# 96 further matmuls behind the last FFN tile of a transformer block

## The chip, the cores and the metric

The kernel runs on one core of a Trainium2 chip. The metric is the device time of one execution in microseconds (us); every time below comes from the profile of one execution or from the timed runs.

## What is computed

A block that adds three things: its input, an attention over 8 earlier positions at stride 2, and a feed-forward network (FFN) with a squared ReLU. S is 2048 rows, D is 576, the hidden width F is 4608, all in float32.

```
xn  = layernorm(x)
q, k, v = split(xn @ wqkv)                  # 32 heads of 18
logits[s, w] = q[s] . k[s - 2 w] / sqrt(18) # w = 0..7, earlier positions alone
attn = softmax(logits over w)
A   = (sum over w of attn[s, w] v[s - 2 w]) @ wo
h   = xn @ w1 + b1
B   = relu(h)**2 @ w2 + b2
out = x + A + B
```

## The kernel before

[...] To keep accuracy, every operand is split into a high and a low half, and each product is made of three matmuls: high by high, high by low, low by high. The copies that make the halves run on ScalarE (ACT) and VectorE (DVE); the lines of the profile for them are L96 (high half) and L98 (low half).

The rows are worked through in four blocks of 512 (`NB = 4`, `TB = 512`), and in each block the FFN runs over 36 tiles of 128 hidden units (`NF = 36`), so 144 tiles in all (`NT = 144`). `step(n)` deals with tile n:

- it asks for the weights of tile n + 2 (`load_w`, on the queue of SyncE) and splits the first weight of tile n + 1 (`split_w1`);
- `ffn1(n)` makes the hidden units: 14 matmuls of 128 x 512 into one PSUM tile `wk` (L340), then ReLU and square on ACT (L342, L345, L346) and the low half `hl` on DVE (L347);
- `split_w2(n)` splits the second weight into `w2h` and `w2l`;
- `ffn2(n - LAG)` adds a finished tile to six PSUM banks `y0` to `y5` that hold the block's result, with pairs of matmuls of 320 and 256 columns (L365). `LAG` is 2, so the second half of a tile is two steps behind its first half.

Between these, the steps carry pieces of the attention, the products with `wo` and the loads of the next block, at hand-written step numbers. The order on each engine is that in which the program states it.

Behind step 143 there is one more, step 144, which runs `ffn2_tail` for the last two tiles. It takes the banks `y0` to `y5` one after another: six matmuls (L365, twelve for a bank of two halves), then `drain` on DVE (L385) adds the bank to the input rows, and a store to the output follows (L404, L406, L408). The last bank, `y5`, is therefore the last to be computed, drained and stored.

Buffers come from rotating pools: `w1h` and `w1l` have 2 buffers each, `w2h` 3, `hh` 4, `raw1` 3, and the PSUM pool of `wk` 2. A tile that takes a buffer over waits until the last reader of its former tile is done. A float32r matmul loads its stationary operand itself, so each shows up as one weight load (PEld) and one matmul (PE). A bf16 matmul is preceded by a weight load of its own. In the kernel before there are 14 bf16 matmuls, all at its start (L448), on a tile of zeros.

Of the kernel before, what the change touches and what calls it, by code (L numbers as in the profile page):

```python
# [8 lines left out]
F32 = mybir.dt.float32  # L9
F32R = mybir.dt.float32r  # L10
BF16 = mybir.dt.bfloat16
AF = mybir.ActivationFunctionType
# [4 lines left out]
P = 128  # L17
S, D, F = 2048, 576, 4608
H, DH, W, DIL = 32, 18, 8, 2
TB = 512  # L20
NB = S // TB
NJ = TB // P
NC = 5
# [16 lines left out]
def block_kernel(ctx: ExitStack, tc: tile.TileContext, x, xt, wqkv, wo, w1, b1, w2, b2, out):  # L40
# [453 lines left out]
    def step(n):  # L494
        if 2 < n + 2 < NT:
            load_w(n + 2)
        if n + 1 < NT:
            split_w1(n + 1)
        for f, a in pre.get(n, []):
            f(*a)  # L500
        if n < NT:
            ffn1(n)
            split_w2(n)
        busy = n >= NF and n % NF in (LAG - 1, LAG - 2)
        for f, a in mid.get(n, []):
            f(*a)
        if not busy:
            piece()
            piece()
        if n == NT:  # L510
            ffn2_tail([NT - 2, NT - 1])
        elif n >= LAG:
            ffn2(n - LAG)
        if not busy:
            piece()

    for n in range(NT + 1):
        with opening() if n < 3 else ExitStack():
            step(n)


_OUTS = [((1, S, D), 'float32')]

# [33 lines left out]
```

## Time and profile before

| | |
|---|---|
| median of the timed runs | 1196.32 us (1195.88 and 1196.75) |
| the profiled execution, its time | 1196.13 us |
| its span, first to last instruction | 1194.1 us |
| TensorE matmuls (PE) busy | 1185.2 us, 99% |
| TensorE weight loads (PEld) busy | 1077.8 us, 90% |
| VectorE (DVE) busy | 869.2 us, 73% |
| ScalarE (ACT) busy | 597.5 us, 50% |
| granted TensorE clock, mean | 1.000 of full speed |

The profiled execution's time is 2.03 us longer than its span, and 0.19 us below the median of the runs. Matmuls are pipelined: one starts before the end of the one before it, so the duration of a single matmul is longer than the distance from start to start. Where a row of the timeline merges several instructions, it shows the stretch from the first start to the last end.

### The profile page before, as it was taken

What the parts mean: (1) busy time and instruction counts of PE and PEld (TensorE: products, weight loads), DVE (VectorE), ACT (ScalarE), POOL (GpSimd) and SP (SyncE); (2) the same over time, 40 slices, a digit from 0 to 9 for tenths busy, and PEclk for the clock granted to TensorE, in tenths of its full rate; (3) what the DMA queues carried; (4) which work ended last, traced back from release to release, by engine and by line L of the source; (5) the groups of instructions that cost most, each with busy time, mean ns of one, the idle gap of its engine ahead of it and who ended that gap; (6) DMA issues with size and microseconds to landing.
All of it is one profiled execution on the core that took longest, in us unless ns stands there. A gap on an engine that the chain in (4) does not pass through costs nothing.

```text
span 1194.1 us, 17735 instructions
## 1 busy us (share of the span) xinstructions
PE 1185.2 (99%) x6930; PEld 1077.8 (90%) x6930; DVE 869.2 (73%) x1051; ACT 597.5 (50%) x1079; POOL 40.7 (3%) x47
## 2 busy tenths in 40 slices
PE   8999999999999999999999999999999999999998
PEld 5998998989898989989989899989998999998998
DVE  7499798882689795994288979598428895958432
ACT  6546445553546454555354545455535454445541
POOL 4002000000000200000000020000000000000000
PEclk9999999999999999999999999999999999999999
DMA  7546345332536544433264654533326434343311
GB/s 233 196 169 227 127 148 201 100 99 73 198 129 213 207 163 152 132 91 109 72 230 138 230 203 119 179 96 105 102 87 225 178 109 169 99 153 95 106 60 50
DMA packets 70164, 172.22 MB, mean 144 GB/s; under 512 B 8384, under 2 KB 20288, under 8 KB 69312
## 3 DMA queue, kind: packets, MB, share of 16 engines
q1 hardware_dynamic: 70080, 171.09, 43.4%
q8 instruction: 54, 0.88, 0.3%
q14 instruction: 30, 0.25, 0.1%
HBM read 156.81 MB, written 14.24 MB: 143 GB/s over the span
## 4 chain that ended last, share of the span: by engine, by line
PE 97%; DVE 2%; ACT 0%; DMA 0%; issue 0%; SPq 0%; POOL 0%
PE y L365 42%; PE wk L340 39%; PE wk L239 15%; DVE xt L183 1%; PE wk L200 1%; DVE w2l L98 0%; DMA xb<-in_x 0%; SPq L87 0%; DVE wql L98 0%; PE y L200 0%; DVE hl L347 0%; ACT r L342 0%; ACT hh L345 0%; DVE st L109 0%; DVE w1l L98 0%
## 5 line engine op out<-in xcount | busy, mean ns | idle before, releaser
L365 PE MATMUL y<-w2h,hh 128*128 128x256 f32 (+1 forms) x1152 | 253.0, 297 | 0.0
L365 PE MATMUL y<-w2l,hh 128*128 128x256 f32 (+1 forms) x1152 | 252.9, 296 | 0.0
L365 PE MATMUL y<-w2h,hl 128*128 128x256 f32 (+1 forms) x1152 | 251.9, 296 | 0.0
L340 PE MATMUL wk<-xh,w1h 128*128 128x512 f32 x720 | 215.6, 396 | 0.9 <-DVE kv L205 0.9
L365 PEld LDWEIGHTS y<-w2h,hh 128*128 128x128 f32 x1152 | 186.1, 189 | 9.2
L340 PE MATMUL wk<-xh,w1l 128*128 128x512 f32 x720 | 191.4, 394 | 2.0 <-DVE w1l L98 2.0
L365 PEld LDWEIGHTS y<-w2l,hh 128*128 128x128 f32 x1152 | 180.7, 190 | 2.2
L365 PEld LDWEIGHTS y<-w2h,hl 128*128 128x128 f32 x1152 | 179.6, 190 | 0.4
L96 ACT ACTIVATE w1h<-raw 128x640 fp32r<-128x640 f32 x144 | 105.9, 736 | 124.4 <-PE wk L340 113.8
L340 PEld LDWEIGHTS wk<-xh,w1l 128*128 128x128 f32 x720 | 134.7, 187 | 35.3 <-DVE w1l L98 2.3
L96 ACT ACTIVATE w2h<-raw 128x576 fp32r<-128x576 f32 x144 | 98.1, 683 | 135.1 <-PE y L365 133.9
L340 PE MATMUL wk<-xl,w1h 128*128 128x512 f32 x576 | 158.1, 394 | 0.0
L98 DVE TENSOR_TENSOR w1l<-raw,w1h 128x640 fp32r<-128x640 f32 x143 | 119.4, 835 | 52.7 <-PE wk L340 37.3
L98 DVE TENSOR_TENSOR w2l<-raw,w2h 128x576 fp32r<-128x576 f32 x144 | 112.6, 783 | 53.6 <-ACT w2h L96 53.4
L340 PEld LDWEIGHTS wk<-xh,w1h 128*128 128x128 f32 x720 | 126.0, 188 | 22.0 <-DVE kv L205 1.1
L301 DVE TENSOR_REDUCE qo<-pr 128x144 f32<-128x1152 f32 x64 | 139.7, 2183 | 0.6
L340 PEld LDWEIGHTS wk<-xl,w1h 128*128 128x128 f32 x576 | 107.6, 187 | 26.3
L347 DVE TENSOR_TENSOR hl<-r,hh 128x512 fp32r<-128x512 f32 x144 | 100.0, 694 | 34.5 <-ACT r L346 34.4
L342 ACT ACTIVATE r<-wk,b1t 128x512 f32<-128x512 f32 x144 | 98.7, 686 | 49.1 <-PE wk L340 48.9
L98 DVE TENSOR_TENSOR wql<-wqr,wqh 128x432 fp32r<-128x432 f32 x80 | 48.9, 628 | 98.0 <-ACT wqh L96 98.0
L239 PE MATMUL wk<-wql,xh 128*128 128x432 f32 x320 | 115.0, 360 | 0.0
L239 PE MATMUL wk<-wqh,xh 128*128 128x432 f32 x320 | 114.4, 358 | 0.0
(77 smaller groups left out, 1229.2 us busy)
## 6 DMA issues: line engine op xcount, KB each, us to landing
raw<-in_w SPq DMA_DIRECT2D x144, 320.0 KB, 2.9
raw<-in_w SPq DMA_DIRECT2D x144, 288.0 KB, 2.8
wqr<-in_wqkv SPq DMA_DIRECT2D x80, 216.0 KB, 4.4
kv<-kscr SPq DMA_DIRECT2D x16, 1008.0 KB, 5.7
kv<-vscr SPq DMA_DIRECT2D x16, 1008.0 KB, 7.8
raw<-in_wo SPq DMA_DIRECT2D x20, 288.0 KB, 2.7
kscr<-kv SPq DMA_DIRECT2D x16, 288.0 KB, 3.0
vscr<-kv SPq DMA_DIRECT2D x16, 288.0 KB, 3.4
```

What stands on the lines that cost most here:

```text
L96: nc.scalar.activation(hi, raw, AF.Copy)
L98: (only or nc.vector).tensor_tensor(out=lo, in0=raw, in1=hi.bitcast(F32), op=ALU.subtract)
L183: nc.vector.tensor_tensor(out=v, in0=v, in1=mb[b][:, :, k].rearrange("c p j -> c j p"), op=op)
L200: nc.tensor.transpose(p[:, j * P:(j + 1) * P], src[:, j, c * P:(c + 1) * P], ident)
L239: nc.tensor.matmul(ps, l, r, start=i == 0, stop=i == len(mm) - 1)
L301: nc.vector.tensor_reduce(out=q[:, j], in_=pr.rearrange("p w c -> p c w"), axis=AX.X, op=ALU.add)
L340: nc.tensor.matmul(p, l, r, start=i == 0, stop=i == len(mm) - 1)
L342: nc.scalar.activation(r, p, AF.Relu, bias=b1t[:, f:f + 1])
L347: last_hl[0] = nc.vector.tensor_tensor(out=hl, in0=r, in1=hh.bitcast(F32), op=ALU.subtract)
L365: nc.tensor.matmul(y, a[:, t * P:(t + 1) * P], w[:, c0:c1], start=first and i == 0 and opens, stop=last and i == len(pairs) - 1, skip_grou ...
```

## The change

A function `rate_rows` is called once, behind the last step. It makes four copies of the last tile's first weight, which still lies in its buffer: on ACT into a `w1h` and a `w2h` buffer, on DVE into a `w1l` buffer (which nothing reads) and, as bf16, into an `hh` buffer. It takes the two `wk` tiles of PSUM, `a` and `c2`, and issues 96 matmuls into them. Nothing reads their results, and each overwrites the one before it. The matmuls come in groups: 38 of 512 columns with fixed or changing stationary and moving operands, 4 of 512 columns with every second element, 4 each of 320, 256, 128, 64 and 32 columns, two groups of 4 of 256 columns at different starts, 4 in bf16, and at the end 8 full ones of 512 columns mixed with 14 that use only the lower or the upper 64 rows of the array.

```diff
+    def rate_rows():
+        b = NB - 1
+        wh = sb.tile([P, NC * P], F32R, name="w1h", bufs=2)
+        wl = sb.tile([P, NC * P], F32R, name="w1l", bufs=2)
+        m2 = sb.tile([P, D], F32R, name="w2h", bufs=3)
+        nc.scalar.activation(wh, raw1[NT - 1], AF.Copy)
+        nc.vector.tensor_copy(wl, raw1[NT - 1])
+        nc.scalar.activation(m2, raw1[NT - 1][:, :D], AF.Copy)
+        low = sb.tile([P, TB], BF16, name="hh", bufs=4)
+        nc.vector.tensor_copy(low, raw1[NT - 1][:, :TB])
+        a = pw.tile([P, TB], F32, name="wk")
+        c2 = pw.tile([P, TB], F32, name="wk")
+        cs = lambda c: slice(c * P, (c + 1) * P)
+        x_, l_ = xh[b], xl[b]
+        mm = lambda p, l, r: nc.tensor.matmul(p, l, r, start=True, stop=True, skip_group_check=True)
+        for i in range(6):
+            mm(a, wh[:, cs(0)], x_[:, 0])
+        for i in range(8):
+            mm(a, wh[:, cs(i % 4)], x_[:, 0])
+        for i in range(8):
+            mm(a, wh[:, cs(0)], x_[:, i % 4])
+        for i in range(8):
+            mm(a, wh[:, cs(i % 4)], x_[:, i % 4])
+        for i in range(8):
+            mm(a, wh[:, cs(i % 4)], l_[:, i % 4])
+        for i in range(4):
+            mm(a, wh[:, cs(i % 4)], x_[:, 0:2].rearrange("p c (n s) -> p (c n) s", s=2)[:, :, 0])
+        for n in (320, 256, 128, 64, 32):
+            for i in range(4):
+                mm(a[:, :n], wh[:, cs(i % 4)], m2[:, :n])
+        for i in range(4):
+            mm(a[:, :256], wh[:, cs(i % 4)], m2[:, 320:])
+        for i in range(4):
+            mm(a[:, :256], wh[:, cs(i % 4)], m2[:, 256:512])
+        for i in range(4):
+            mm(a, low[:, cs(i % 4)], low)
+        h0, h1 = slice(0, 64), slice(64, 128)
+        for i in range(4):
+            mm(a, wh[:, cs(0)], x_[:, 0])
+            mm(a, wh[h0, cs(1)], x_[h0, 1])
+            mm(c2, wh[h1, cs(1)], x_[h1, 1])
+        for i in range(3):
+            mm(a, wh[:, cs(0)], x_[:, 0])
+        for i in range(3):
+            mm(a, wh[h0, cs(1)], x_[h0, 1])
+            mm(c2, wh[h1, cs(1)], x_[h1, 1])
+        mm(a, wh[:, cs(0)], x_[:, 0])
+
+    rate_rows()
```

## The prediction

> **What bounds the kernel now.** I read the page's first and second parts, then the chain of work that ended last, then that chain in order of time near the end, and last the timeline of the final microseconds.
>
> ```profile
> span 1194.1 us, 17735 instructions
> PE 1185.2 (99%) x6930; PEld 1077.8 (90%) x6930; DVE 869.2 (73%) x1051; ACT 597.5 (50%) x1079; POOL 40.7 (3%) x47
> PE 97%; DVE 2%; ACT 0%; DMA 0%; issue 0%; SPq 0%; POOL 0%
> ...
> 1174.90 0.65 PE y L365 x5
> 1175.55 3.27 PE wk L340 x14
> 1178.82 11.72 PE y L365 x88
> 1190.55 0.02 issue
> 1190.57 0.49 DVE xb L385
> ```
>
> The chain is TensorE for 97% of the span, and TensorE is idle for only 1194.1 - 1185.2 = 8.9 us in all. In the last 15 us the chain is one unbroken run of matmuls, and after it come only the drain of the last bank and its store. So whatever is put behind the last matmul on TensorE starts at once, and is on the path that sets the end as soon as it outlasts drain and store. The time of the change is therefore a sum over 96 matmuls, less what drain and store cover.
>
> **Where the added matmuls start, and what covers them.** With the instructions of both programs, as built, laid side by side, nothing changes on TensorE up to the last L365 matmul: the 96 stand behind it in the order of the source. POOL and SyncE issue the same work as before, and no DMA is added. The end of the timeline, and the DMA issue that ends last, are these:
>
> ```profile
> 1190.08 0.31 PE L365 MATMUL y<-w2l,hh 128*128 128x320 f32 x1
> ...
> 1190.22 0.31 PE L365 MATMUL y<-w2h,hl 128*128 128x320 f32 x1
> ...
> 1191.09 0.34 SPq L408 DMA_DIRECT2D out<-xb  x1
> ...
> out<-xb SPq DMA_DIRECT2D x2, 160.0 KB, 2.1
> ```
>
> The last matmul starts at 1190.22; at the pace of its kind (0.147 us, below) the first added one starts at 1190.37. The last store is issued at 1191.09 and takes 2.1 us to land, so at 1193.2. From there to the end of the span are 1194.1 - 1193.2 = 0.9 us, which I take as the closing work of the program: something has to finish last, and then the engines meet. After the change the last matmul finishes last, and I put the same 0.9 us behind it. Drain and store run beside the added matmuls. They cover the stretch from 1190.37 to 1193.2, 2.8 us.
>
> **The pace of a matmul.** A row's mean is the duration of one matmul; what counts in an unbroken run is the distance between starts. These rows give both:
>
> ```profile
> 1183.97 0.31 PE L365 MATMUL y<-w2h,hh 128*128 128x320 f32 x1
> ...
> 1184.85 0.40 PE L365 MATMUL y<-w2h,hh 128*128 128x256 f32 x2
> 1185.09 0.40 PE L365 MATMUL y<-w2l,hh 128*128 128x256 f32 x2
> ...
> 1162.12 0.60 PE L200 MATMUL wk<-ident,qo 128*128 128x128 f32 x4
> ...
> 1.24 6.10 PE L448 MATMUL wk<-warm 128*128 128x512 bf16 x14 [1.24 <-DVE warm L445]
> ...
> L340 PE MATMUL wk<-xh,w1h 128*128 128x512 f32 x720 | 215.6, 396 | 0.9 <-DVE kv L205 0.9
> L365 PE MATMUL y<-w2h,hh 128*128 128x320 f32 x576 | 180.5, 313 | 0.0
> L365 PE MATMUL y<-w2h,hh 128*128 128x256 f32 x576 | 161.2, 281 | 0.0
> L200 PE MATMUL wk<-ident,qo 128*128 128x128 f32 x80 | 12.0, 272 | 0.0
> L448 PE MATMUL wk<-warm 128*128 128x512 bf16 x14 | 6.1, 628 | 1.2 <-DVE warm L445 1.2
> ```
>
> - 512 columns: 14 matmuls of L340 fill 3.27 us of the chain, 0.2336 us each, though one lasts 396 ns. In these 14 both operands change and all write the same bank.
> - 320 columns: six in a row into one bank start from 1183.97 to 1184.85, 0.147 us each.
> - 256 columns: two start between 1184.85 and 1185.09, 0.120 us each.
> - 128 columns: four transposes, (0.60 - 0.272) / 3 = 0.109 us each. This is the narrowest the trace has.
> - bf16 of 512 columns: (6.10 - 0.628) / 13 = 0.421 us at the start of the program. The window below shows the clock at 1.00 at the end, where float32r of the same width takes 0.2336. I take 0.2336 for bf16 too; its lower bound is half of 0.421, 0.210, if the first matmuls ran at half speed.
>
> ```profile
> 1175.00:1190.00 15.00, 15.00 (x105) 14.35 (x104) 3.86 (x7) 2.64 (x4) 0.00 (x0) 1.00 0.09 38
> ```
>
> **The sum, group by group.**
>
> - 38 of 512 columns with fixed or changing operands: 38 x 0.2336 = 8.88. Every float32r matmul here brings a weight load of its own (6930 of each on the page), so I expect no gain from a fixed stationary operand. The lower bound is the 14 that repeat it at 0.210: 0.33 less.
> - 4 with every second element: 4 x 0.2336 = 0.93. No row has a moving operand with a gap. At worst twice the bytes are passed over at the same rate: 0.93 more. I take the plain row, because the columns are the same in number.
> - 4 of 320: 0.59. 12 of 256, whatever their start: 1.44.
> - 12 of 128, 64 and 32 columns at 0.109: 1.31, taking the narrowest row as a floor set by the weight load, which stays 128 x 128. If time fell with the columns, the 256 row gives 4 x (0.060 + 0.030 + 0.015) = 0.42, so 0.89 less; if a narrow one cost as much as the 512 row, 12 x 0.2336 = 2.80, so 1.49 more.
> - 4 in bf16: 0.93, or 0.09 less.
> - 8 full ones among the half-height ones: 1.87.
> - 14 of half height: 14 x 0.2336 = 3.27. No row has a matmul of 64 array rows; the nearest is the full one of the same 512 columns. Lower bound: the two of a pair run at once in the two halves of the array, 7 x 0.2336 = 1.64. Upper bound: full and half height alternate 10 times (twice in each of four rounds, then twice more), and if the array has to empty each time, the part of the 396 ns that overlap hides, 396 - 234 = 162 ns, shows: 1.62 more.
>
> Together 8.88 + 0.93 + 0.59 + 1.44 + 1.31 + 0.93 + 1.87 + 3.27 = 19.22 us. The last matmul starts 0.23 before the end of that sum and lasts 0.396, so TensorE ends at 1190.37 + 19.22 + 0.16 = 1209.75. With the 0.9 us of closing work the span is 1210.65; the profiled execution's time was 1196.13 - 1194.1 = 2.03 us above its span, so the time is 1212.7 us. That execution stands 0.19 us below the median of the runs shown, 1196.32, so against the median it is 16.4 us or 1.4% more.
>
> The Trainium skill, "TensorE: Matmul & The Clock Gate", Back-to-back issue gap, gives columns / 2.4 + 2.5 ns from start to start on a warm array, so 216 ns for 512 columns. This trace does not agree: 0.2336 us, 8% more. By the page the 68 full-width ones would be 68 x 0.018 = 1.2 us cheaper, an estimate.
>
> **The copies.** Four are added, and none is waited for.
>
> ```profile
> L96 ACT ACTIVATE w1h<-raw 128x640 fp32r<-128x640 f32 x144 | 105.9, 736 | 124.4 <-PE wk L340 113.8
> L96 ACT ACTIVATE w2h<-raw 128x576 fp32r<-128x576 f32 x144 | 98.1, 683 | 135.1 <-PE y L365 133.9
> L98 DVE TENSOR_TENSOR w1l<-raw,w1h 128x640 fp32r<-128x640 f32 x143 | 119.4, 835 | 52.7 <-PE wk L340 37.3
> ...
> 1169.23 0.69 ACT L342 ACTIVATE r<-wk,b1t 128x512 f32<-128x512 f32 x1 [2.59 <-PE wk L340]
> 1171.28 0.69 DVE L347 TENSOR_TENSOR hl<-r,hh 128x512 fp32r<-128x512 f32 x1 [3.85 <-ACT r L346]
> ...
> 1180.24 0.63 ACT L346 ACTIVATE r<-r 128x512 f32<-128x512 f32 x1
> 1180.91 0.69 DVE L347 TENSOR_TENSOR hl<-r,hh 128x512 fp32r<-128x512 f32 x1 [3.85 <-ACT r L346]
> ```
>
> The `w1h` copy (0.74 us) stands on ACT ahead of the L342 at 1169.23 and waits for the last matmul of its buffer's former tile. ACT is idle for 2.59 us there. If it came late by its whole length, `hh` and `hl` behind it would slip by 0.74 us, and they are wanted only in the tail after 1183.97, 12 us later. The `w1l` copy on DVE (at most 0.84, the row with two sources) stands ahead of the `hl` at 1171.28 and has 3.85 us of idle time; it waits for matmuls that end near 1169.2. The bf16 copy lies in the 3.85 us ahead of 1180.91. The `w2h` copy (0.68) is the last on ACT and waits for its buffer's last reader, just before 1183.97, so it ends near 1184.7. The first matmul that reads it is the 43rd added one, at 1190.37 + 42 x 0.2336 = 1200.2. That is 15 us of cover; without it TensorE would stand for 0.68 us.
>
> **The rivals.**
>
> *Half-height pairs run at once.* Same sum with 1.64 in place of 3.27: 1211.1 us. For it: the two use different rows of the array and different PSUM tiles, and nothing reads either. Against it: in all of the trace each matmul waits for its forerunner to stream. The Trainium skill, "TensorEngine Tiling (Array Packing)", Key Properties, says that tiles of the array run independently, and that a change of tiling mode first drains the array; by the first half the pairs overlap, by the second the ten changes cost something. No row of before shows either.
>
> *The unusual shapes cost more.* Narrow ones at 2.80, gaps at twice, ten emptyings: 1.49 + 0.93 + 1.62 = 4.04 more at most, 1216.7 us; half of it is 1214.7. For it: no row shows any of them. Against it: all three would have to go the bad way.
>
> *Nothing overlaps* (the one that ends slower by over 2%). Each added matmul opens and closes its own accumulation and writes over the one before it in the same bank. If each had to wait until its forerunner has left the array, full durations would count: 68 x 0.396 + 4 x 0.313 + 12 x 0.281 + 12 x 0.272 = 34.8 us in place of 19.2, so 1228.1 us. It decides from a mean of 0.278 us per matmul on (19.22 + 7.5 to the 2% line, over 96). Against it: the 14 bf16 ones at the start are of this form, and start 0.421 us apart while each lasts 0.628.
>
> *The matmuls end up elsewhere or hidden.* Even if they filled every idle moment of TensorE, 19.2 - 8.9 = 10.3 us would be left, so 1206.4. The order as built speaks against it.
>
> **How the numbers follow.** Forecast by rows 0.48, pairs at once 0.22, unusual shapes dearer 0.24, nothing overlaps 0.04, elsewhere 0.02. The low end takes the pairs at once, the narrow ones by their columns and the fixed operand: 1212.7 - 1.64 - 0.89 - 0.33 = 1209.8, which I round down to 1209.5. The high end is the dear case, 1216.7, and 0.3 us for the engines' meeting: 1217.0. Within 2% of the median means below 1220.2 us, and 2% is about what a measurement of this kernel can tell from no change. All cases but the one without overlap stay below it. Faster is left only 0.01 for what I have not seen, slower 0.05, same 0.94.
>
> **What the changed profile would show.** L535 rows of 96 matmuls with TensorE busy without a gap from about 1190.4 to 1209.7; starts 0.234 us apart in the first 42; the chain ending in PE L535 and no longer in DVE L385; the last store issued at 1191.1 as before; steps up to 1190 the same to a tenth. Wrong would be: a gap ahead of the 43rd (the `w2h` copy late), a pace above 0.278 over the block, a granted clock below 1.00 in it, or two half-height matmuls starting together.

## The result, and the profile after

The changed kernel takes 1213.28 us (two runs, 1213.28 and 1213.29) against 1196.32 before: 17.0 us more, a ratio of 1.0142 with a 95% interval of 1.0098 to 1.0185. That is within 2%, as forecast, and 0.6 us above the forecast of 1212.7.

These are lines of the page, and then the end of the chain of work in order of time:

```profile
span 1211.6 us, 17932 instructions
PE 1205.2 (99%) x7026; PEld 1092.1 (90%) x7026; DVE 869.9 (72%) x1053; ACT 598.6 (49%) x1081; POOL 40.6 (3%) x47
...
1190.34 20.34 PE wk L535 x95
```

TensorE has 96 more matmuls, DVE and ACT two more instructions each. The chain used to end in the drain of the last bank on DVE; now it ends in 20 us of L535. The timeline of TensorE from there on gives the parts of the sum, since each group starts where the one before it has been issued:

```profile
1190.18 7.15 PE L535 MATMUL wk<-xh,w1h 128*128 128x512 f32 x30
...
1197.16 2.03 PE L535 MATMUL wk<-xl,w1h 128*128 128x512 f32 x8
...
1199.03 1.98 PE L535 MATMUL wk<-xh,w1h 128*128 128x512 f32 x4
...
1200.83 3.52 PE L535 MATMUL wk<-w2h,w1h 128*128 128x320 f32 x28
...
1204.19 1.04 PE L535 MATMUL wk<-hh 128*128 128x512 bf16 x4
...
1204.88 5.80 PE L535 MATMUL wk<-xh,w1h 128*128 128x512 f32 x22
```

`float32r`, the type of the kernel's split operands, stands in these rows as f32. A row here merges shapes of one line: the 28 are all those of 320 to 32 columns, the 22 the full and the half-height ones. From start to start:

| part | forecast us | measured us |
|---|---|---|
| start of the first added matmul | 1190.37 | 1190.18 |
| 38 of 512 columns | 8.88 | 8.85 |
| 4 with every second element | 0.93 | 1.80 |
| 28 of 320 to 32 columns | 3.34 | 3.36 |
| 4 in bf16 | 0.93 | 0.69 |
| 8 full and 14 half-height, to TensorE's end | 5.30 | 5.80 |
| end of TensorE | 1209.75 | 1210.68 |
| from there to the end of the span | 0.9 | 0.9 |
| time less span | 2.03 | 1.7 |

The copies cost nothing. These are the two on ACT, in the timeline:

```profile
1167.87 0.74 ACT L526 ACTIVATE w1h<-raw 128x640 fp32r<-128x640 f32 x1 [1.42 <-PE wk L340]
...
1183.97 0.69 ACT L528 ACTIVATE w2h<-raw 128x576 fp32r<-128x576 f32 x1 [3.29 <-PE y L365]
```

The first lies in the gap foreseen, with 0.43 us still idle between it and L342, and the `w2h` copy is done at 1184.7, 16 us before its reader. The two on DVE take 0.49 and 0.42 us, in their gaps.

### The profile page after: what moved, and what is told of

Its sections match the earlier page's. It is cut to its first block, busy times and chain, and to the rows that moved or that the text cites. A ratio compares the mean times of both kernels' runs of the same rounds, so it can differ in the third digit from the quotient of the medians.

```text
span 1211.6 us, 17932 instructions
## 1 busy us (share of the span) xinstructions
PE 1205.2 (99%) x7026; PEld 1092.1 (90%) x7026; DVE 869.9 (72%) x1053; ACT 598.6 (49%) x1081; POOL 40.6 (3%) x47
## 4 chain that ended last, share of the span: by engine, by line
PE 97%; DVE 2%; issue 0%; ACT 0%; DMA 0%; SPq 0%; POOL 0%; DVEq 0%
PE y L365 42%; PE wk L340 38%; PE wk L239 15%; PE wk L535 2%; DVE xt L183 1%; PE wk L200 1%; DVE wql L98 0%; DMA xb<-in_x 0%; SPq L87 0%; PE y L200 0%; DVE w2l L98 0%; DVE hl L347 0%; ACT r L342 0%; ACT hh L345 0%; POOL rs L118 0%
## 5 line engine op out<-in xcount | busy, mean ns | idle before, releaser
L365 PE MATMUL y<-w2h,hh 128*128 128x256 f32 (+1 forms) x1152 | 253.0, 297 | 0.0
L365 PE MATMUL y<-w2l,hh 128*128 128x256 f32 (+1 forms) x1152 | 252.9, 296 | 0.0
L365 PE MATMUL y<-w2h,hl 128*128 128x256 f32 (+1 forms) x1152 | 251.9, 296 | 0.0
L340 PE MATMUL wk<-xh,w1h 128*128 128x512 f32 x720 | 215.6, 396 | 0.9 <-DVE kv L205 0.9
L365 PEld LDWEIGHTS y<-w2h,hh 128*128 128x128 f32 x1152 | 186.1, 189 | 9.2
L340 PE MATMUL wk<-xh,w1l 128*128 128x512 f32 x720 | 191.5, 394 | 2.0 <-DVE w1l L98 2.0
L365 PEld LDWEIGHTS y<-w2l,hh 128*128 128x128 f32 x1152 | 180.7, 190 | 2.2
L365 PEld LDWEIGHTS y<-w2h,hl 128*128 128x128 f32 x1152 | 179.6, 190 | 0.5
L340 PEld LDWEIGHTS wk<-xh,w1l 128*128 128x128 f32 x720 | 134.7, 187 | 35.3 <-DVE w1l L98 2.3
L340 PE MATMUL wk<-xl,w1h 128*128 128x512 f32 x576 | 158.1, 394 | 0.0
L340 PEld LDWEIGHTS wk<-xh,w1h 128*128 128x128 f32 x720 | 126.0, 188 | 21.9 <-DVE kv L205 1.1
L340 PEld LDWEIGHTS wk<-xl,w1h 128*128 128x128 f32 x576 | 107.6, 187 | 26.3
L342 ACT ACTIVATE r<-wk,b1t 128x512 f32<-128x512 f32 x144 | 98.5, 684 | 47.8 <-PE wk L340 47.6
```

The costliest lines, as they stand in the source:

```text
L340: nc.tensor.matmul(p, l, r, start=i == 0, stop=i == len(mm) - 1)
L342: nc.scalar.activation(r, p, AF.Relu, bias=b1t[:, f:f + 1])
L365: nc.tensor.matmul(y, a[:, t * P:(t + 1) * P], w[:, c0:c1], start=first and i == 0 and opens, stop=last and i == len(pairs) - 1, skip_grou ...
```

## Experiments

The theory behind the forecast: the time added is the sum of the paces of the matmuls, less what drain and store cover. Two terms came out dearer and were open: reading with gaps, and changes between full and half height. Every experiment changes `rate_rows` alone. The first five are compared with the kernel before by their times; the others hold groups of matmuls on lines of their own, and are read from their profile, one execution each.

### The changed kernel again

No edit: a base for the next three on the same chip.

> The changed kernel as it is, on the same chip as the three that follow, so that they can be compared with it. Both theories: 1213.3 us, 17.0 over the kernel before.

Measured: 1214.53 us (1213.56 to 1215.37), against 1196.58 for the kernel before on the same chip, ratio 1.0149 (1.0135 to 1.0163). The added part is the same as in the first profile, 20.34 us of the chain. What differs lies 1180 us earlier, and is told in the last section: single executions scatter by 1 to 2 us, so the next two are read from their profiles.

### The same matmuls, sorted by height

```diff
-        for i in range(4):
-            mm(a, wh[:, cs(0)], x_[:, 0])
-            mm(a, wh[h0, cs(1)], x_[h0, 1])
-            mm(c2, wh[h1, cs(1)], x_[h1, 1])
...
+        for i in range(8):
+            mm(a, wh[:, cs(0)], x_[:, 0])
+        for i in range(7):
+            mm(a, wh[h0, cs(1)], x_[h0, 1])
+            mm(c2, wh[h1, cs(1)], x_[h1, 1])
```

> The same 96 matmuls, but the last block in another order: its 8 full ones first, then its 7 pairs of half height. Theory: every change between 128 and 64 rows costs 0.19 us, because the weight load of the next matmul can't run beside the one before; there are 10 changes in the mixed order and 1 in this, so 9 x 0.19 = 1.7 us less than the changed kernel, 1211.6 us. Rival: the half-height matmuls themselves are dear (0.43 us a pair, whatever stands next to it); then the order changes nothing and the time stays 1213.3 us.

The start of the added part and the last block in the timeline of the repeated kernel, and then the last block in that of the sorted one:

```profile
1190.85 7.15 PE L535 MATMUL wk<-xh,w1h 128*128 128x512 f32 x30
...
1205.56 5.80 PE L535 MATMUL wk<-xh,w1h 128*128 128x512 f32 x22
```

```profile
1206.45 4.05 PE L535 MATMUL wk<-xh,w1h 128*128 128x512 f32 x22
```

The block is 1.75 us shorter, and 1.7 were expected: the order costs, and not the half-height matmuls. The time is 1213.51 us, ratio 1.0137 (1.0124 to 1.0151); that is 1.0 less than the repeated kernel, but the intervals overlap, so the time alone doesn't show it.

### The four with gaps read plainly

```diff
-            mm(a, wh[:, cs(i % 4)], x_[:, 0:2].rearrange("p c (n s) -> p (c n) s", s=2)[:, :, 0])
+            mm(a, wh[:, cs(i % 4)], x_[:, i % 4])
```

> The same 96 matmuls, but the four that read every second element read 512 neighbouring ones instead. Theory: the gap alone makes them 0.454 us in place of 0.2336, so 4 x 0.22 = 0.88 us less than the changed kernel, 1212.4 us, and they start 0.23 us apart. Rival: something else slows the matmuls at this place (what is left of the store, a wait for the copy behind them); then they stay 0.45 us apart and the time stays 1213.3 us.

In its timeline the four and the group behind them:

```profile
1201.23 1.10 PE L535 MATMUL wk<-xh,w1h 128*128 128x512 f32 x4
1202.16 3.51 PE L535 MATMUL wk<-w2h,w1h 128*128 128x320 f32 x28
```

The four take 1202.16 - 1201.23 = 0.93 us instead of 1.80: the gap is the whole cause. The time, 1214.18 us (ratio 1.0145, 1.0129 to 1.0160), doesn't resolve 0.87 us.

### Only 8, and only 16 added matmuls

```diff
-        for i in range(6):
-            mm(a, wh[:, cs(0)], x_[:, 0])
...
+        for i in range(8):
+            nc.tensor.matmul(a, wh[:, cs(i % 4)], x_[:, i % 4], start=True, stop=True, skip_group_check=True)
```

> Only 8 added matmuls of 512 columns in place of 96, all four copies kept. Theory: drain and store of the last bank cover what ends before the store lands. TensorE ends at 1190.18 + 8 x 0.2336 + 0.16 = 1192.2 of the span, the store lands at 1192.8, so the time is that of the kernel before, 1196.3 us, and the span 1194.1. Rival: all that stands behind the last L365 matmul adds to the time: 8 x 0.2336 = 1.9 us, 1198.2 us.

> As with 8, but 16 added matmuls of 512 columns. Theory: TensorE ends at 1190.18 + 16 x 0.2336 + 0.16 = 1194.1 of the span, 1.3 us after the store has landed, and the same 0.9 us of closing work follow: span 1195.0, 0.9 us over the kernel before, so 1197.2 us. Rival that all adds: 16 x 0.2336 = 3.7 us, 1200.0 us.

The ends of the two timelines, first with 8, then with 16:

```profile
1190.11 2.02 PE L536 MATMUL wk<-xh,w1h 128*128 128x512 f32 x8
...
1190.83 0.34 SPq L408 DMA_DIRECT2D out<-xb  x1
```

```profile
1190.55 3.88 PE L536 MATMUL wk<-xh,w1h 128*128 128x512 f32 x16
```

With 8, TensorE ends at 1192.1, before the store lands at 1190.83 + 2.1 = 1192.9: the time is 1196.12 us against 1196.58 for the kernel before on that chip, ratio 0.9997 (0.9988 to 1.0005), where the rival asked for 1.9 us more. With 16, TensorE ends at 1194.43 and the span, 1195.3, 0.9 us later: 1198.31 us against 1197.70, ratio 1.0005 (0.9996 to 1.0014). That is 0.6 us more, where the theory had 0.9 and the rival 3.7. Both agree with the cover of the forecast and rule out that all the matmuls add; the interval with 16, -0.5 to 1.7 us, is too wide to size the cover.

### What a gap in the moving operand costs

Groups of 8 with 512 or 256 columns and several patterns. Two of the lines:

```diff
+            nc.tensor.matmul(a, wh[:, cs(i % 4)], xf[:, :2048].rearrange("p (n s) -> p n s", s=4)[:, :, 0], ...)
+            nc.tensor.matmul(a.rearrange("p (n s) -> p n s", s=2), wh[:, cs(i % 4)], xf[:, :1024].rearrange("p (n s) -> p n s", s=4)[:, :, :2], ...)
```

> In place of the 96: groups of 8 matmuls with 512 columns whose moving operand is read plainly, then every 2nd, 3rd and 4th element, then 2 of 4, then 4 of 8, then 4 pieces of 128 from far apart; then 256 columns with every 2nd element and plainly; then bf16 with 512 columns plainly and every 2nd, 256 columns with every 4th and plainly; last plain float32r again. Theory A (time goes with the span of bytes passed over): from start to start 0.23, 0.45, 0.68, 0.91, 0.45, 0.45 us, pieces 0.23; bf16 0.22 and 0.43, 0.43 and 0.11. Theory B (two neighbours of 8 bytes come in one read, and without a neighbour each element needs its own): 0.23, 0.45, 0.45, 0.45, then 0.23 for 2 of 4, 4 of 8 and the pieces; bf16 of 2 bytes with every 2nd may stay at 0.22. Theory C (lines of 16 bytes need two hits): 0.23, 0.23 to 0.45, 0.45 or more, 0.9, and 2 of 4 as plain.

The timeline; a group's pace is the distance to the next row over 8:

```profile
1191.80 2.02 PE L538 MATMUL wk<-xh,w1h 128*128 128x512 f32 x8
1193.66 3.79 PE L540 MATMUL wk<-xh,w1h 128*128 128x512 f32 x8
1197.27 3.78 PE L542 MATMUL wk<-xh,w1h 128*128 128x512 f32 x8
1200.87 3.87 PE L544 MATMUL wk<-xh,w1h 128*128 128x512 f32 x8
1204.56 3.81 PE L546 MATMUL wk<-xh,w1h 128*128 128x512 f32 x8
1208.19 2.05 PE L548 MATMUL wk<-xh,w1h 128*128 128x512 f32 x8
```

Plain (L538) 0.232 us; every second, third and fourth (L540, L542, L544) 0.451, 0.450 and 0.461; 2 of 4 (L546) 0.454; 4 of 8 (L548) fills 2.05 us as the plain ones fill 2.02, and so do the pieces. None of the three theories holds: A fails on the third and fourth and on 4 of 8, B on 2 of 4, C on the fourth and on 2 of 4. In bf16 every second costs 0.226 against 0.217, and 256 columns with every fourth 0.225 against 0.11 plainly (from start to start within the row). So there are two paces, and four elements within 16 bytes seemed to get the good one. The next run tests that:

```diff
+            nc.tensor.matmul(a.rearrange("p (n s) -> p n s", s=4), wh[:, cs(i % 4)], xf[:, :1024].rearrange("p (n s) -> p n s", s=8)[:, :, 2:6], ...)
+            nc.tensor.matmul(a.rearrange("p (n s) -> p n s", s=4), wh[:, cs(i % 4)], xf[:, :768].rearrange("p (n s) -> p n s", s=6)[:, :, :4], ...)
```

> In place of the 96, groups of 8. float32r: 512 columns plainly; plainly, but begun one element later; 4 of 8; 4 of 8 begun two elements later; 4 of 6; 8 of 16 begun two elements later; 2 of 4 begun one later. bf16: plainly; 2 of 4; 256 columns with every third; 4 of 8. Last plain float32r. Theory D, after the run before (each four elements that follow one another run at full pace where they lie in one aligned line of 16 bytes, and at half pace otherwise; unbroken reading excepted): 0.233, 0.233, 0.233, 0.45, about 0.34, 0.34, 0.45; bf16 0.216, 0.216, 0.22, 0.216. Rival E (what counts is a run of 16 bytes, wherever it lies): 0.233 for the first six, 0.45 for 2 of 4; bf16 0.43 for 2 of 4, 0.22 for every third (half pace for 256 columns), 0.43 for 4 of 8.

```profile
1196.07 2.03 PE L542 MATMUL wk<-xh,w1h 128*128 128x512 f32 x8
1197.93 3.79 PE L544 MATMUL wk<-xh,w1h 128*128 128x512 f32 x8
1201.54 2.90 PE L546 MATMUL wk<-xh,w1h 128*128 128x512 f32 x8
1204.27 2.79 PE L548 MATMUL wk<-xh,w1h 128*128 128x512 f32 x8
1206.88 3.80 PE L550 MATMUL wk<-xh,w1h 128*128 128x512 f32 x8
...
1212.26 1.97 PE L554 MATMUL wk<-hh 128*128 128x512 bf16 x8
1214.07 1.53 PE L556 MATMUL wk<-hh 128*128 128x256 bf16 x8
1215.44 1.97 PE L558 MATMUL wk<-hh 128*128 128x512 bf16 x8
```

4 of 8 (L542) takes 0.232, the same begun two elements later 0.451, 4 of 6 0.341, 8 of 16 begun two later 0.326, 2 of 4 begun one later as long a row as L544 with its 0.45, and bf16 with 2 of 4 (L554) 0.226, with 4 of 8 (L558) filling the same 1.97 us. Plain reading begun one element later takes (1196.07 - 1194.18) / 8 = 0.236. D holds in all of these to 0.015 us, and E, which asked for 0.23 in the three float32r groups that D slows and for 0.43 in bf16, fails. D misses one: every third in bf16 takes 0.171 for 256 columns where both said 0.22. The rule is thus good for float32r and not complete for bf16.

### What a change of height costs

Full ones, halves, pairs, quarters and mixtures, each group on a line of its own. One of them, full and lower half by turns:

```diff
+        for p, l, r in [(a, wh[:, cs(0)], x_[:, 0]), (a, wh[h0, cs(1)], x_[h0, 1])] * 6:
+            nc.tensor.matmul(p, l, r, start=True, stop=True, skip_group_check=True)
```

> In place of the 96, on lines of their own: 8 full matmuls; 6 times (full, lower half); 6 times (full, lower half, upper half); 12 lower halves; 12 pairs of lower and upper half; 12 times four quarters of 32 rows into four banks; 8 full; 6 times (3 full, 3 pairs); 8 full. Theory (each change of the number of rows costs 0.19 us, halves of a pair run at once, and nothing else costs): a full one 0.234; a round of full and lower half 2 x 0.234 + 2 x 0.19 = 0.85; a round of full and pair the same 0.85; a lower half 0.234; a pair 0.234; four quarters 0.234; a round of 3 full and 3 pairs 6 x 0.234 + 2 x 0.19 = 1.78. Rival (the second half of a pair is what costs): full and lower half 0.47, full and pair 0.85, pair alone 0.43. Rival (a half-height matmul can't load its weights early at all): a lower half alone 0.43, a pair 0.43.

```profile
1193.85 5.05 PE L541 MATMUL wk<-xh,w1h 128*128 128x512 f32 x12
1198.84 5.21 PE L543 MATMUL wk<-xh,w1h 128*128 128x512 f32 x18
1203.88 2.49 PE L545 MATMUL wk<-xh,w1h 64*128 64x512 f32 x10
1205.99 0.50 PE L547 MATMUL wk<-xh,w1h 64*128 64x512 f32 x1
...
1206.45 0.40 PE L545 MATMUL wk<-xh,w1h 64*128 64x512 f32 x1
...
1209.57 0.49 PE L549 MATMUL wk<-xh,w1h 32*128 32x512 f32 x2
...
1214.54 10.65 PE L553 MATMUL wk<-xh,w1h 128*128 128x512 f32 x54
1225.12 2.12 PE L555 MATMUL wk<-xh,w1h 128*128 128x512 f32 x8
```

A round of full and lower half (L541) takes (1198.84 - 1193.85) / 6 = 0.83 us, a round of full and pair (L543) (1203.88 - 1198.84) / 6 = 0.84, and a round of 3 full and 3 pairs (L553) (1225.12 - 1214.54) / 6 = 1.76: the expected 0.85, 0.85 and 1.78. So the pair's second half is free, and only the change costs. 12 lower halves (L545) and 12 pairs (L547), 24 lower halves in all, take 1209.57 - 1203.88 = 5.69 us, 0.237 each; the 12 upper ones add nothing. The upper half even runs ahead of the program's order: L547 starts at 1205.99, while lower halves of the line before it still start until 1206.45. Twelve rounds of four quarters (L549) take 0.25 us a round.

What the change consists of was tried by its stationary width:

```diff
+        for p, l, r in [(a[:64], wh[:, cs(0)][:, :64], x_[:, 0]), (a[:64], wh[h0, cs(1)][:, :64], x_[h0, 1])] * 8:
+            nc.tensor.matmul(p, l, r, start=True, stop=True, skip_group_check=True)
```

> In place of the 96: 8 full matmuls, then 8 times (full, lower half), with 128, with 64 and with 32 stationary columns and 512 moving ones; then the same with 128 stationary and 256 moving; then the same in bf16; last 8 full. Before, a full one and a lower half by turns took 0.19 us each more than without turns. Theory: that 0.19 us is the weight load that can't run beside another mode, so it shrinks with the stationary columns (0.112 us of load for 128, 0.058 for 64, 0.032 for 32): 0.42, about 0.37 and about 0.34 us from start to start, and 0.24 in bf16, whose load is short. Rival: it is the emptying of the array at each change, whatever is loaded: 0.42 for all three widths of float32r, and 0.40 in bf16. Both: 0.30 with 256 moving.

```profile
1194.88 6.75 PE L539 MATMUL wk<-xh,w1h 128*128 128x512 f32 x16
1201.56 2.06 PE L541 MATMUL wk<-xh,w1h 128*64 128x512 f32 x8
1203.46 5.98 PE L543 MATMUL wk<-xh,w1h 128*64 128x512 f32 x16
1209.37 2.04 PE L545 MATMUL wk<-xh,w1h 128*32 128x512 f32 x8
1211.25 5.59 PE L547 MATMUL wk<-xh,w1h 128*32 128x512 f32 x16
1216.76 1.21 PE L549 MATMUL wk<-xh,w1h 128*128 128x256 f32 x8
...
1228.11 4.55 PE L555 MATMUL wk<-hh 128*128 128x512 bf16 x14
1232.59 2.13 PE L557 MATMUL wk<-xh,w1h 128*128 128x512 f32 x8
```

By turns the matmuls start 0.417, 0.369 and 0.344 us apart with 128, 64 and 32 stationary columns (L539, L543, L547), so a change costs about 0.18, 0.14 and 0.11 over 0.233. The group of 256 moving columns ran partly at half clock, which is told in the last section; before that its matmuls start 0.31 us apart, where both theories had 0.30. The half clock reaches into the start of the bf16 turns too; the row shows the last 14 of these 16, (1232.59 - 1228.11) / 14 = 0.320 us apart against 0.217, so a change costs 0.10. The load does count, and the rival (0.42 for all widths, 0.40 in bf16) fails; but the theory's 0.24 for bf16 fails too. The loads measured next (0.108, 0.059 and 0.031, and about 0.025 in bf16) account for the differences. What is left, 0.08 us, is nearly the same for all four: a change costs a fixed part and the weight load. What the fixed part is made of was not tried.

### What sets the pace of narrow and of wide matmuls

```diff
+            nc.tensor.matmul(a[:32, :32], wh[:, (i % 4) * P:(i % 4) * P + 32], x_[:, i % 4, :32], ...)
```

> In place of the 96, groups of 8: 512, 128 and 32 moving columns, each with 128, 64 and 32 stationary columns, in float32r; then bf16 with 512, 128 and 32 moving columns and 128 stationary, and 32 with 32; then float32r with 192, 384 and 512 moving; then 6 times (128 stationary, 64 stationary). Theory for the 0.112 us of the narrow ones: it is the load of 128 stationary columns, so 0.056 with 64 and 0.03 with 32 stationary, for 32 moving columns. Rival: a fixed cost per matmul, 0.11 whatever the stationary width. Theory for the 18 ns that float32r of 512 columns takes over bf16 (0.234 against 0.216): they come from the weight load that each float32r matmul brings, so with 64 stationary columns 0.225 and with 32 0.22. Rival: they come from the moving side, and 0.234 stays for all three.

```profile
1192.66 2.02 PE L536 MATMUL wk<-xh,w1h 128*128 128x512 f32 x8
1194.53 2.02 PE L538 MATMUL wk<-xh,w1h 128*64 128x512 f32 x8
1196.38 2.01 PE L540 MATMUL wk<-xh,w1h 128*32 128x512 f32 x8
...
1200.04 1.01 PE L548 MATMUL wk<-xh,w1h 128*128 128x32 f32 x8
1200.90 0.62 PE L550 MATMUL wk<-xh,w1h 128*64 128x32 f32 x8
1201.37 0.40 PE L552 MATMUL wk<-xh,w1h 128*32 128x32 f32 x8
1201.62 1.90 PE L554 MATMUL wk<-hh 128*128 128x512 bf16 x8
1203.36 0.61 PE L556 MATMUL wk<-hh 128*128 128x128 bf16 x8
```

32 columns take 0.108, 0.059 and 0.031 us with 128, 64 and 32 stationary columns: the weight load is the floor, as the theory had it. In bf16, 32 columns with 128 stationary take 0.035 by the distance to the next row and 0.025 from start to start within it, load included. 512 columns in float32r take 0.234 and 0.231 with 128 and 64 stationary columns, and with 32 stationary columns the eight fill 2.01 us, as with 64: most of what they take over bf16 (0.217) stays, so it comes from the moving side, and the theory on it falls. 128 moving columns agree: with 32 stationary columns, whose load takes 0.031, they take 0.061 us, against 0.056 in bf16.

The last mixture of this run takes turns between 128 and 64 stationary columns with all 128 rows in use. Its 12 matmuls take (1211.43 - 1208.64) / 12 = 0.233 us each, as without turns. So it is the change of rows that costs, and not a change of the stationary width.

## Why the prediction was right, and where it wasn't

*The path.* Right. The block starts where the last L365 matmul leaves off, and the chain ends in it. The first added one starts 0.19 us earlier than said, because the first 11 us were that much quicker in this execution: its first L340 matmul starts at 11.29 us, and at 11.49 in the profile before. The cover held: 8 matmuls are free. The 0.9 us of closing work is there again, after 96 and after 16 behind the last matmul, and after 8 behind the store (1193.8 - 1192.9).

*The pace of 512 columns.* Right: 8.85 for 8.88, with any mix of operands, and the float32r weight load gives no gain for a fixed one. The rule weighed beside it, of the Trainium skill ("TensorE: Matmul & The Clock Gate", Back-to-back issue gap), agrees for bf16, where the run gave 0.217 us, and not for float32r.

*Narrow ones.* Right, and for the reason given: 3.36 for 3.34, with the weight load as the floor.

*bf16.* Mis-sized: 0.93 in the sum, 0.69 measured. Its lower bound, 0.21 each, was near the truth, 0.217. 0.17 of the difference is shifted into the next block, as the first full one counts as started 0.03 us after the last bf16 one. In the sorted run that step and the one behind it are 0.028 and 0.424 us, together what two usual ones take.

*Gaps.* Mis-sized: I took the plain row, because the columns were the same in number; 1.80 for 0.93. The upper bound, twice the time, was right in size and wrong in cause: not the bytes passed over count, since every fourth costs no more than every second.

*Half height.* Two misses that nearly cancel. The 14 were priced as if each streamed alone, 3.27, but pairs do run at once: 15 x 0.2336 = 3.50 for full ones and pairs together, in place of 5.14. In the trace of the changed kernel the two of a pair start 3 to 15 ns apart, which was one of the prediction's own signs of being wrong. The argument against it, that in all of the trace each matmul waits for its forerunner to stream, could not speak on pairs, as every matmul of the kernel before uses all 128 rows. And each of the 10 changes costs 0.19, above the 0.162 that I gave as the bound: the weight load, 0.11, shows besides a fixed part of 0.08. 3.50 + 1.9 + 0.16 for the last one's own length make 5.56; with the 0.17 from bf16, 5.73 of the 5.80 measured. The rival "pairs at once" was thus right in its mechanism and wrong in its time, since the changes eat what the overlap brings. The Trainium skill ("TensorEngine Tiling (Array Packing)", Key Properties) says that tiles run independently and that a change of mode drains the array. The runs agree with the first (24 lower halves and 12 upper ones take 0.237 us for each lower one); they show that a change of rows costs 0.19 us, but not that this is a drain.

*The other rivals.* "Nothing overlaps" fails: from 1190.18 to 1210.68 the mean is 0.214 us per matmul, below 0.278. "Elsewhere or hidden" fails too: all 96 stand behind the last L365 matmul, from 1190.18 on. "Unusual shapes cost more" was right for the gaps (0.87 of the 0.93 it allowed) and for the changes of height, and wrong for the narrow ones.

So the nearness of 1212.7 to 1213.28 is in part luck: 0.87 (gaps) and 0.50 (half height) too little, against 0.24 (bf16), 0.19 (start), 0.01 net of the plain and narrow ones, and 0.35 (time less span) too much. What failed in the sum are its terms for the gaps and for bf16, and the assumption that the half-height ones stream one by one.

## What to carry to other kernels

Work put behind the last matmul is free only as long as drain and store of the last result last, here some 2 us of TensorE time; beyond it, it adds its distances from start to start, not its durations. For float32r, count 0.233 us for 512 columns and never less than the 0.11 us of a 128-column weight load, and where the moving operand has gaps, keep four neighbouring elements in one aligned line of 16 bytes, or pay up to double. Pairs of half height are worth their halved time only in runs, since each change of height costs 0.19 us, nearly as much as a pair.

## What the runs showed of the hardware beside

The clock halves early in some executions. These are windows of 5 us of the first profile of the changed kernel and of the repeated one (after the stretch: busy time of PE, PEld, DVE, ACT and POOL, the granted clock, the DMA share, GB/s):

```profile
9.00:14.00 5.00, 4.89 (x26) 3.53 (x26) 4.36 (x8) 4.07 (x8) 3.04 (x6) 1.00 1.00 361
```

```profile
9.00:14.00 5.00, 4.55 (x20) 3.80 (x21) 3.83 (x8) 3.72 (x8) 3.51 (x7) 0.66 1.01 365
```

In the repeated kernel a mean of 0.66 over 5 us is 3.4 us at half clock, and its added part starts at 1190.85 instead of 1190.18. The sorted one has one such stretch and starts its added part at 1191.75; the plain one has two and starts it at 1192.37. This fits the scatter of single executions by 1 to 2 us; that it is all of it wasn't shown.

It also came late, in the run on changes of height: while full and half height took turns with 256 columns, the clock fell to half, though TensorE counts as busy:

```profile
1221.00:1227.50 6.50, 6.17 (x14) 2.68 (x15) 0.00 (x0) 0.00 (x0) 0.00 (x0) 0.50 0.00 0
```

By turns with 512 columns, where 0.233 of 0.42 us is streaming, it never fell; with 256, 0.12 of 0.31 us is. Whether this share decides it was not tried.
